# Attention in chunks, then a SoLU feed-forward: the opening's order of steps listed anew, g by another queue, two units of w_out scaled in place

## The chip, the cores and the metric

The kernel runs on one core of a Trainium2 chip. Its time is device time in microseconds (us), the median of the timed runs. Five engines each work through a list of instructions of their own, in order: TensorE (PE in the profile), VectorE (DVE), ScalarE (ACT), GpSimd (POOL) and SyncE (SP), which only issues transfers. An instruction waits until what it reads is written and what it overwrites is read.

## The reference

```python
# attention inside chunks of 64 tokens; batch 8, heads 8, seq 576, head_dim 64
scores = (1 / sqrt(D)) * q_c @ k_c.T          # per chunk and head, 64 x 64
attn = softmax(scores);  out = attn @ v_c
x = out with heads side by side               # 4608 tokens x 512
# feed-forward
h = x @ w_in                                  # 512 -> 1024
sm = softmax(h);  solu = h * sm
ln = (solu - mean(solu)) / sqrt(var(solu) + 1e-6) * g_ln
result = ln @ w_out                           # 1024 -> 512
```

w_in, w_out and g_ln are as they come; the weights reach the kernel as 64-bit floats and are turned into 32-bit ones on the chip.

## The kernel before

The 4608 tokens are 36 tiles of 128, two chunks each. A tile goes through: load q, k, v; q and k transposed; scores; softmax; attention transposed; values (which gives x transposed); product with w_in; SoLU; z transposed; product with w_out; store. Most products are taken in pieces: an operand is split into a high part of the float32r type and what is left of it, and three products (low weight, high, low of the data) add up in PSUM. Tiles 0 and 1 multiply the full 32-bit weights by plain float32 instead (FM = 2), before the parts exist.

**Units of weights.** w_in comes as units 0 to 3, w_out as units 4 to 7, 1 MB each. `load_pair` (line 144, step P) issues the transfer, unit 0 in two halves (P0, P1). `unit_scale` (167, step c) clamps the upper word, on VectorE or GpSimd, and then scales it on ScalarE. `unit_round` (183, step C) shifts by three bits and then adds the lower word, both on VectorE. `unit_high` (200, step t) writes the high part on ScalarE; for w_out it is multiplied by g on the way. `unit_rest` (213, step D:unit:half) writes what is left, on GpSimd for the halves in SUB_POOL (two instructions for w_out, a multiplication by g and a subtraction), else on VectorE in one.

**Steps of a tile.** n loads q and k, v loads v. N:i:0 and N:i:1 transpose q and k of tile i on TensorE into a PSUM bank, and the step's second mention copies the bank out (VectorE for the pairs in NV_DVE, else ScalarE). S: scores. A: VectorE takes the maximum and subtracts, the second mention has ScalarE's exponential. B: sum and reciprocal on VectorE, second mention the normalization (GpSimd for the tiles in NORM_POOL). T: attention transposed, then copied out. V: values on TensorE, then x copied out by ScalarE, the third mention the low part by VectorE. M: product with w_in (M:0 in four mentions, a unit each). X: VectorE's maximum of the product, then ScalarE's exponential. Y: VectorE's product, then an affine pass by ScalarE, or GpSimd for the tiles in MEAN_POOL. R: variance. z:i:x: half of z transposed on TensorE, high part by ScalarE, low part by VectorE. F: a third of an output product. o: store. Z, U, K, Q, q: the later tiles' transposes by VectorE and their loads. W: two small products on the identity that nothing reads. g loads the vector g, G transposes it and writes it for use.

**The order.** The opening, up to tile 4, is the string START (line 19): its words are called in order (line 815), each word being a step; a step with several parts goes one part on at each mention. Every engine gets its instructions in the order in which the words make them; that order is kept. Two words on different engines do not wait for each other unless data or a buffer ties them. PSUM gives the copies, transposes and output products two banks in turn (`bank`, line 116); `ph` holds one product with w_in at a time, so M of a tile follows the last read of the tile before, by Y. From tile 5 on a loop (line 838) makes one tile a turn; the change does not touch it.

Of the kernel before, what the change touches and what calls it, by code (L numbers as in the profile page):

```python
# [12 lines left out]
AF = mybir.ActivationFunctionType  # L13
# [3 lines left out]


START = """
W:41 W:42 n:0 n:1 N:0:1 N:0:0 N:0:0 N:0:1 N:1:0 n:2 S:0 N:2:1 N:1:0 A:0 A:0 P0 P1 P:2 N:1:1 B:0  # L20
P:1 c:0 c:2 N:1:1 W:43 c:0 N:2:0 S:1 W:44 W:45 W:46 N:2:1 N:2:0 n:3 c:2 C:0 A:1 A:1 C:0 B:0 c:1
B:1 S:2 T:0 N:3:0 T:0 W:47 g W:4 c:1 N:3:0 A:2 v:0 C:2 N:3:1 P:3 G P:4 t:0 V:0 N:3:1 n:4 C:1 B:1
G V:0 A:2 S:3 C:1 C:2 T:1 B:2 B:2 c:3 c:3 M:0 t:2 M:0 A:3 C:3 T:1 M:0 v:1 A:3 C:3 c:4 B:3 M:0
N:4:1 X:0 t:1 N:4:0 c:4 n:5 N:4:1 T:2 v:2 B:3 N:4:0 n:6 X:0 V:1 C:4 v:3 P:5 P:6 D:1:0 T:2 Y:0
S:4 T:3 C:4 N:5:0 V:1 A:4 t:3 A:4 P:7 T:3 D:1:1 M:1 t:4 N:5:1 D:3:1 B:4 D:2:1 N:5:0 D:0:1 D:2:0
D:0:0 Y:0 N:5:1 V:2 N:6:1 D:3:0 v:4 D:4:0 N:6:0 c:5 B:4 D:4:1 V:2 S:5 X:1 n:7 N:6:1 X:1 V:2 Y:1
z:0:1 N:6:0 V:3 z:0:1 c:5 R:0 A:5 z:0:0 C:5 A:5 z:0:0 V:3 C:5 M:2 z:0:1 T:4 c:6 B:5 z:0:0 V:3
Q:2 S:6 t:5 c:6 N:7:0 T:4 X:2 C:6 V:4 q:8 v:5 N:7:0 B:5 n:8 D:5:1 c:7 D:5:0 T:5 X:2 Y:2 C:6 T:5
F c:7 Y:2 t:6 C:7 N:7:1 C:7 N:7:1 D:6:1 D:6:0 M:3 F t:7 D:7:0 A:6 V:4 N:8:0 V:4 D:7:1 R:2 q:8
Y:1 N:8:0 V:5 S:7 X:3 Z:2 X:3 N:8:1 Y:3 A:7 N:8:1 A:6 q:8 q:8 F z:1:0 z:1:0 R:1 A:7 B:6 v:6  # L30
z:1:0 M:4 V:5 B:7 B:6 Y:3 U:6 o:0 B:7 Z:3 z:1:1 U:7 z:1:1 v:7 X:4 o:0 X:4 F z:1:1 Y:4 R:3 F K:9
F o:1 Y:4 o:1 V:5 R:4
"""


# [23 lines left out]
def chunk_attention_then_solu_ffn(  # L59
# [10 lines left out]
    nc = tc.nc  # L70

    B, H, S, D = q.shape
    DM, FF = H * D, g_ln.shape[0]
    P = 128
# [3 lines left out]
    G = S // 32  # L78
# [4 lines left out]
    assert FF == 32 * 32  # L83


    NV_DVE = ((0, 1), (1, 0), (2, 1), (4, 0), (6, 1), (9, 1),)
    MEAN_POOL = (3, 4,)
    CL_DVE = (0, 3, 4,)
    TV_DVE = (3,)
    SUB_POOL = ((0, 0), (0, 1), (1, 0), (1, 1), (2, 0), (2, 1), (3, 0), (3, 1), (7, 0), (7, 1),)  # L90
    NORM_POOL = (0, 1, 2, 3, 4, 5, 6, 7,)
    SH_POOL = ()
    XV_DVE = ()
    FM = 2
    MS = nc.gpsimd
    ORD = 5
# [12 lines left out]
    pe, dve, act, pool, sync = (  # L109
        order.engine(e)  # L110
        for e in (nc.tensor, nc.vector, nc.scalar, nc.gpsimd, nc.sync)
    )
# [12 lines left out]
    g_sb = const.tile([P, NFC], F32, name="g_sb")  # L125
    g_row = const.tile([NFC, P], F32, name="g_row")
# [40 lines left out]
    def unit_scale(x):  # L167
# [32 lines left out]
    def unit_high(x):  # L200
        kind, m = UNITS[x]
        a = scaled[x]
        if kind == "in":
            top = wi_h[:, m, :].rearrange("p (x n) -> p x n", x=2)
            act.copy(top, a)
        else:
            top = wo_h[:, 2 * m:2 * m + 2, :]
            for y in range(2):
                g = g_sb[:, 2 * m + y:2 * m + y + 1]
                act.activation(top[:, y], a[:, y], AF.Copy, scale=g)  # L210
        tops[x] = top

    def unit_rest(x, y):

        kind, m = UNITS[x]
        a, top = scaled[x], tops[x]
        g = None
        if kind == "in":
            low = wi_l[:, m, y * HALF:(y + 1) * HALF]
        else:  # L220
            low = wo_l[:, 2 * m + y, :]
            g = g_sb[:, 2 * m + y:2 * m + y + 1]
        of, part = a[:, y], top[:, y].bitcast(F32)
        if (x, y) in SUB_POOL:
            if g is not None:
                pool.tensor_scalar(out=of, in0=of, scalar1=g, scalar2=None, op0=ALU.mult)
            pool.tensor_tensor(out=low, in0=of, in1=part, op=ALU.subtract)
        elif g is None:
            dve.tensor_tensor(out=low, in0=of, in1=part, op=ALU.subtract)
        else:  # L230
            dve.scalar_tensor_tensor(
                out=low, in0=of, scalar=g, in1=part, op0=ALU.mult, op1=ALU.subtract
            )
# [5 lines left out]
    QT, KT, V, QS, KS = {}, {}, {}, {}, {}  # L239
# [98 lines left out]
    def turn_natural(i, x):  # L338
# [25 lines left out]
    def attn(i, part):  # L364
        return (sx, sy)[i % 2 if order.on else part][:, :, part]
# [46 lines left out]
    def softmax_b(i):  # L412
# [15 lines left out]
    def attn_transpose(i):  # L428
# [148 lines left out]
    def solu_b(i):  # L577
# [8 lines left out]
        yield  # L586
        if i not in MEAN_POOL:
            act.activation(z, z, AF.Identity, scale=-float(FF), bias=zsum)
# [156 lines left out]
        sync.dma_start(*early[1])  # L745

    def load_g():
        sync.dma_start(g_row, g_ln.rearrange("(a p) -> a p", p=P))

    def turn_g():  # L750
        pt = bank()[:, :NFC]
# [48 lines left out]
    def product():  # L800
# [135 lines left out]
```

## Time and profile before

| what | value |
|---|---|
| median of 3 runs | 476.63 us (476.55 to 477.74) |
| the profiled execution | 477.58 us, span 475.8 us |
| TensorE | busy 463.6 us, 97% of the span |
| VectorE | 369.1 us, 78% |
| ScalarE | 250.0 us, 53% |
| GpSimd | 160.8 us, 34% |
| chain that ended last | PE 91%, DVE 3%, DMA 2%, SyncE's queue 2% |

Busy time is the time in which an engine has an instruction under way. The span runs from the first instruction to the last, and the device's time has a little around it. A row of the timeline gives start, duration, engine, operation, what is written from what, shapes, the count of merged instructions, and in brackets the idle time before with what ended it. The program's names are those of the code: `w_a` is a unit being worked, `wi_l`/`wo_l` what is left of w_in/w_out, `wi_h`/`wo_h` the high parts, `po` a bank, `sx` the scores, `sy` the values, `ph` the product with w_in. Every row has line 50, since a helper at that line records every instruction.

### The profile page before, as it was taken

The numbers are of one execution on the slowest core, as the hardware profiler recorded it, in microseconds if no ns is written. First come the engines' busy times: TensorE is split into PE (matmuls) and PEld (weight loads), VectorE is DVE, ScalarE is ACT, GpSimd is POOL, SyncE is SP. The second block draws the span as 40 slices with busy tenths as digits, with TensorE's granted clock in tenths as the row PEclk, the third lists the DMA queues.
The fourth block names the chain that finished last, engine by engine and source line by source line (L and its number), as shares of the span: only waits on it lengthen the run. The fifth ranks groups of instructions, "written<-read, shape, count | busy, mean of one in ns | idle before, by whom it ended". The sixth has DMA issues, their size and how long they took to land.

```text
span 475.8 us, 10988 instructions
## 1 busy us (share of the span) xinstructions
PE 463.6 (97%) x4193; PEld 379.1 (80%) x4193; DVE 369.1 (78%) x511; ACT 250.0 (53%) x402; POOL 160.8 (34%) x305
## 2 busy tenths in 40 slices
PE   6799999999999999999999999999999999999996
PEld 5655888888888888888888888888888888888876
DVE  2799988798888787878788878787879797944430
ACT  2565885546464646464545454555555555554451
POOL 0438557350505050505050505032505050513300
PEclk9899999999999999999999999999999999999999
DMA  9999887877887877687358596959644435433211
GB/s 227 299 246 312 159 141 143 200 181 155 184 159 174 155 179 139 161 161 171 82 143 162 136 174 157 178 131 179 150 106 118 105 95 129 110 89 112 67 44 45
DMA packets 192996, 72.05 MB, mean 151 GB/s; under 512 B 177128, under 2 KB 177648, under 8 KB 192560
## 3 DMA queue, kind: packets, MB, share of 16 engines
q1 hardware_dynamic: 186528, 58.63, 55.4%
q0 software_dynamic: 6272, 12.60, 10.1%
q8 instruction: 33, 0.54, 0.5%
q14 instruction: 19, 0.16, 0.1%
q10 hardware_dynamic: 144, 0.13, 0.1%
HBM read 36.70 MB, written 9.44 MB: 97 GB/s over the span
## 4 chain that ended last, share of the span: by engine, by line
PE 91%; DVE 3%; DMA 2%; SPq 2%; issue 1%; ACT 0%; DVEq 0%; ACTq 0%
PE po L50 42%; PE ph L50 41%; PE sx L50 4%; PE sy L50 3%; DMA nat_z<-in_q_dram 2%; SPq L50 2%; DVE w_a L50 1%; DVE h_nmax L50 0%; DVE z L50 0%; ACT z L50 0%; DVE e L50 0%; DVE qT L50 0%; ACT z_h L50 0%; DVE s_nmax L50 0%; DVE s_sum L50 0%
## 5 line engine op out<-in xcount | busy, mean ns | idle before, releaser
L50 PE MATMUL po<-wo_l,z_h 128*128 128x512 f32 x280 | 110.9, 396 | 0.1
L50 PE MATMUL po<-wo_h,z_l 128*128 128x512 f32 x280 | 109.3, 391 | 0.0
L50 PE MATMUL po<-wo_h,z_h 128*128 128x512 f32 x280 | 109.3, 390 | 0.0
L50 ACT ACTIVATE z<-ph,h_nmax 128x1024 f32<-128x1024 f32 x36 | 40.2, 1116 | 131.6 <-DVE h_nmax L50 131.5
L50 PE MATMUL ph<-wi_l,x_h 128*128 128x512 f32 x272 | 106.1, 390 | 0.0
L50 PE MATMUL ph<-wi_h,x_h 128*128 128x512 f32 x272 | 105.8, 389 | 0.0
L50 POOL TENSOR_TENSOR u<-ssq,eps 128x1 f32<-128x1 f32 x36 | 6.8, 190 | 218.9 <-ACT sq L50 218.9
L50 POOL DMA_DIRECT2D z_t<-z_b x136 | 67.9, 506 | 16.6 <-DVE z_b L50 11.6
L50 PE MATMUL ph<-wi_h,x_l 128*128 128x512 f32 x272 | 72.7, 389 | 0.0
L50 DVE TENSOR_REDUCE h_nmax<-ph 128x1 f32<-128x1024 f32 x36 | 44.0, 1222 | 34.7 <-PE ph L50 34.7
L50 PEld LDWEIGHTS po<-wo_l,z_h 128*128 128x128 f32 x280 | 52.5, 188 | 11.9 <-ACT z_h L50 0.5
L50 PEld LDWEIGHTS po<-wo_h,z_l 128*128 128x128 f32 x280 | 52.6, 188 | 11.3 <-DVE z_l L50 0.4
L50 PEld LDWEIGHTS po<-wo_h,z_h 128*128 128x128 f32 x280 | 52.6, 188 | 10.4
L50 PEld LDWEIGHTS ph<-wi_l,x_h 128*128 128x128 f32 x272 | 51.1, 188 | 10.8 <-issue 0.2
L50 PEld LDWEIGHTS ph<-wi_h,x_l 128*128 128x128 f32 x272 | 51.0, 188 | 10.6
L50 PEld LDWEIGHTS ph<-wi_h,x_h 128*128 128x128 f32 x272 | 51.1, 188 | 10.5
L50 DVE TENSOR_TENSOR z_l<-z_t,z_h 128x1024 fp32r<-128x1024 f32 (+1 forms) x35 | 40.8, 1164 | 20.7 <-ACT z_h L50 20.7
L50 DVE SCALAR_TENSOR_TENSOR z<-ph,z 128x1024 f32<-128x1024 f32 x36 | 44.1, 1224 | 15.0 <-ACT z L50 15.0
L50 ACT ACTIVATE z<-z,z_sum 128x1024 f32<-128x1024 f32 x34 | 39.2, 1153 | 22.7 <-DVE z L50 21.6
L50 DVE STREAM_TRANSPOSE z_b<-z 128x1024 f32<-128x1024 f32 x33 | 39.9, 1210 | 6.1 <-ACT z L50 3.1
L50 ACT ACTIVATE o_sb<-po,r 128x512 f32<-128x512 f32 (+1 forms) x36 | 24.3, 675 | 28.4 <-POOL r L50 20.8
L50 ACT ACTIVATE sq<-z 128x1024 bf16<-128x1024 f32 x36 | 37.5, 1043 | 2.5 <-POOL z L50 2.5
(88 smaller groups left out, 624.5 us busy)
## 6 DMA issues: line engine op xcount, KB each, us to landing
out_dram<-o_sb SPq DMA_DIRECT2D x35, 256.0 KB, 2.5
z_t<-z_b SPq DMA_DIRECT2D x128, 64.0 KB, 3.1
z_t<-z_b POOLq DMA_DIRECT2D x128, 64.0 KB, 2.8
q_st<-in_q_dram SPq DMA_DIRECT2D x96, 72.0 KB, 3.2
k_st<-in_k_dram SPq DMA_DIRECT2D x96, 72.0 KB, 2.8
v_sb<-in_v_dram SPq DMA_DIRECT2D x27, 256.0 KB, 4.4
w_raw<-in_moe_w_out_dram SPq DMA_DIRECT2D x4, 1024.0 KB, 7.9
attn_t<-a_b POOLq DMA_DIRECT2D x60, 64.0 KB, 3.5
```

The lines of the kernel that those rows point to most:

```text
L50: ins = make(*args, **kwargs)
```

## The change

START is replaced as a whole by another order of the same 262 words (each word as often as before). The first transfers become: q and k of tile 0, unit 1, tile 1, unit 0, tile 2, unit 2, v of tile 0, unit 3, tile 3. Before they were tiles 0, 1, 2, units 0, 2, 1, tile 3, g, v of tile 0, unit 3. The lists that choose engines change with it. g is loaded by ScalarE's queue instead of SyncE's. For units 4 and 7 (GM_ACT) ScalarE multiplies the unit by g in place and then copies it to the high part, and the rest is a plain subtraction.

```diff
 START = """
-W:41 W:42 n:0 n:1 N:0:1 N:0:0 N:0:0 N:0:1 N:1:0 n:2 S:0 N:2:1 N:1:0 A:0 A:0 P0 P1 P:2 N:1:1 B:0
-P:1 c:0 c:2 N:1:1 W:43 c:0 N:2:0 S:1 W:44 W:45 W:46 N:2:1 N:2:0 n:3 c:2 C:0 A:1 A:1 C:0 B:0 c:1
-B:1 S:2 T:0 N:3:0 T:0 W:47 g W:4 c:1 N:3:0 A:2 v:0 C:2 N:3:1 P:3 G P:4 t:0 V:0 N:3:1 n:4 C:1 B:1
...
+n:0 N:0:0 P:1 c:1 N:0:1 N:0:0 n:1 P0 P1 N:0:1 S:0 W:41 c:1 n:2 N:1:0 W:45 A:0 P:2 v:0 N:1:0
+N:1:1 C:1 A:0 N:1:1 W:44 P:3 C:1 n:3 W:43 S:1 t:1 n:4 W:42 n:5 B:0 B:0 T:0 T:0 A:1 c:0
+W:47 W:46 A:1 B:1 c:0 B:1 N:2:0 W:4 C:0 c:2 N:2:1 N:2:0 N:2:1 C:0 V:0 v:1 c:2 V:0 P:5 S:2
+A:2 T:1 v:3 t:0 A:2 D:1:1 g c:3 c:5 c:3 M:0 T:1 C:2 C:2 M:0 C:3 C:3 N:3:0 M:0 N:3:1
+N:3:0 N:3:1 D:0:0 N:4:0 B:2 M:0 t:3 B:2 N:4:1 N:4:0 S:3 N:4:1 N:5:0 X:0 X:0 A:3 T:2 N:5:0 V:1 V:1
+S:4 P:4 v:2 Y:0 A:4 n:6 A:3 B:3 N:5:1 T:2 M:1 P:6 B:3 n:7 Y:0 R:0 z:0:0 N:5:1 A:4 Q:2
+B:4 t:2 D:2:0 D:1:0 T:3 c:5 D:2:1 C:5 C:5 X:1 z:0:0 B:4 T:3 V:2 z:0:0 v:4 S:5 G G v:5
+c:4 D:3:0 V:2 X:1 V:2 z:0:1 Y:1 N:6:0 N:6:0 A:5 z:0:1 c:4 t:5 C:4 C:4 D:0:1 P:7 V:3 V:3 V:3
+N:6:1 D:3:1 c:6 M:2 N:6:1 z:0:1 c:6 D:5:1 T:4 N:7:1 D:5:0 t:4 C:6 S:6 X:2 T:4 A:5 D:4:0 X:2 D:4:1
+B:5 B:5 Y:2 c:7 V:4 V:4 N:7:1 F q:8 T:5 Y:2 M:3 Y:1 c:7 T:5 C:6 C:7 t:6 D:6:0 C:7
+t:7 D:6:1 A:6 v:6 q:8 Z:2 q:8 N:7:0 N:7:0 F n:8 q:8 V:4 D:7:0 A:6 D:7:1 X:3 z:1:0 z:1:0 F
...
-    NV_DVE = ((0, 1), (1, 0), (2, 1), (4, 0), (6, 1), (9, 1),)
-    MEAN_POOL = (3, 4,)
-    CL_DVE = (0, 3, 4,)
-    TV_DVE = (3,)
-    SUB_POOL = ((0, 0), (0, 1), (1, 0), (1, 1), (2, 0), (2, 1), (3, 0), (3, 1), (7, 0), (7, 1),)
-    NORM_POOL = (0, 1, 2, 3, 4, 5, 6, 7,)
+    NV_DVE = ((5, 1), (8, 0), (9, 1))
+    MEAN_POOL = (2, 3, 4)
+    CL_DVE = (1, 7)
+    TV_DVE = ()
+    GM_ACT = (4, 7)
+    SUB_POOL = ((0, 1), (1, 0), (2, 0), (3, 0), (3, 1), (4, 1), (5, 0), (6, 0), (7, 0))
+    NORM_POOL = (0, 1, 4, 5, 6)
-    XV_DVE = ()
+    XV_DVE = (0,)
...
-                act.activation(top[:, y], a[:, y], AF.Copy, scale=g)
+                act.activation(
+                    a[:, y] if x in GM_ACT else top[:, y], a[:, y], AF.Copy, scale=g
+                )
+            if x in GM_ACT:
+                act.copy(top, a)
...
-            g = g_sb[:, 2 * m + y:2 * m + y + 1]
+            if x not in GM_ACT:
+                g = g_sb[:, 2 * m + y:2 * m + y + 1]
...
-        sync.dma_start(g_row, g_ln.rearrange("(a p) -> a p", p=P))
+        nc.scalar.dma_start(g_row, g_ln.rearrange("(a p) -> a p", p=P))
```

## Rows read from the trace of the kernel before

**Rows 1.** Busy time by stretch: stretch, length, each engine's busy us, clock, DMA.

```profile
23.58:83.45 59.87, 58.24 (x582) 42.67 (x581) 54.36 (x74) 43.03 (x71) 36.67 (x37) 0.99 0.90 201
83.45:455.00 371.55, 371.48 (x3348) 307.11 (x3347) 298.75 (x414) 192.07 (x309) 117.74 (x253) 1.00 0.63 142
```

**Rows 2.** TensorE in order of time, 20 to 84 us.

```profile
20.34 0.63 PE L50 MATMUL po<-ident,nat_z 128*128 128x128 f32 x4 [2.42 <-DMA nat_z<-in_q_dram]
...
22.39 1.06 PE L50 MATMUL po<-ident,nat_z 128*128 128x128 f32 x4
...
23.58 1.02 PE L50 MATMUL sy<-attn_t,v_sb 64*64 64x64 f32 x32
...
38.01 7.10 PE L50 MATMUL ph<-w_a,x_f 128*128 128x512 f32 x16 [0.94 <-DVE z L50]
...
46.11 1.09 PE L50 MATMUL po<-ident,nat 128*128 128x128 f32 x8
47.13 0.69 PE L50 MATMUL sx<-kT,qT 64*64 64x64 f32 x32
47.76 0.66 PE L50 MATMUL po<-ident,z 128*128 128x128 f32 x4
...
49.65 0.47 PE L50 MATMUL ph<-wi_l,x_h 128*128 128x512 f32 x1
...
55.20 0.60 PE L50 MATMUL po<-ident,e 128*128 128x128 f32 x4
...
83.45 0.39 PE L50 MATMUL ph<-wi_l,x_h 128*128 128x512 f32 x1
```

**Rows 3.** Busy time by stretch, the last two numbers: DMA share, GB/s.

```profile
4.00:8.00 4.00, 2.74 (x12) 2.28 (x12) 0.69 (x1) 0.59 (x1) 0.00 (x0) 1.00 1.38 218
12.00:17.00 5.00, 4.47 (x77) 3.80 (x78) 4.28 (x8) 2.91 (x4) 1.94 (x2) 1.00 0.98 398
18.00:21.00 3.00, 0.66 (x6) 0.69 (x7) 2.83 (x6) 1.60 (x2) 2.35 (x2) 0.99 0.84 146
```

**Rows 4.** SyncE's queue in order of time: start, time to issue.

```profile
13.74 3.63 SPq L50 DMA_DIRECT2D g_row<-in_moe_g_ln_dram  x1
```

**Rows 5.** VectorE in order of time, 34 to 45 us.

```profile
34.90 1.82 DVE L50 TENSOR_SCALAR w_a<-w_a 128x1024 uint32<-128x1024 uint32 x1
...
37.79 2.29 DVE L50 SCALAR_TENSOR_TENSOR w_a<-w_raw,w_a 128x1024 uint16<-128x1024 uint32 x1
...
44.11 1.76 DVE L50 SCALAR_TENSOR_TENSOR wo_l<-w_a,g_sb,wo_h 128x512 fp32r<-128x512 f32 x1
```

**Rows 6.** GpSimd in order of time, single instructions at 35.2 and 39.5 us.

```profile
34.90 1.27 POOL L50 TENSOR_TENSOR wi_l<-w_a,wi_h 128x512 fp32r<-128x512 f32 x1
...
38.84 2.33 POOL L50 TENSOR_TENSOR wi_l<-w_a,wi_h 128x512 fp32r<-128x512 f32 x1
```

**Rows 7.** VectorE in order of time, 45 to 58 us.

```profile
45.79 1.21 DVE L50 TENSOR_REDUCE h_nmax<-ph 128x1 f32<-128x1024 f32 x1
...
49.42 0.69 DVE L50 TENSOR_REDUCE s_nmax<-sx 128x8 f32<-128x512 f32 x1
...
50.82 0.68 DVE L50 TENSOR_SCALAR w_a<-w_a 128x1024 uint32<-128x1024 uint32 x1
51.54 1.37 DVE L50 SCALAR_TENSOR_TENSOR w_a<-w_raw,w_a 128x1024 uint16<-128x1024 uint32 x1
52.78 0.69 DVE L50 TENSOR_TENSOR z_l<-po,z_h 128x512 fp32r<-128x512 f32 x1
...
57.14 1.41 DVE L50 SCALAR_TENSOR_TENSOR wo_l<-w_a,g_sb,wo_h 128x512 fp32r<-128x512 f32 x2
```

**Rows 8.** ScalarE in order of time, 29 to 32 us.

```profile
29.64 0.58 ACT L50 COPY attn_t<-po 128x512 f32<-128x512 f32 x1
30.11 0.63 ACT L50 ACTIVATE e<-e 128x512 f32<-128x512 f32 x1
30.64 1.04 ACT L50 CAST wi_h<-w_a 128x1024 fp32r<-128x1024 f32 x1
```

More of the change, by code (lines that the diff above doesn't have):

```diff
@@ L19 @@
 START = """
-W:41 W:42 n:0 n:1 N:0:1 N:0:0 N:0:0 N:0:1 N:1:0 n:2 S:0 N:2:1 N:1:0 A:0 A:0 P0 P1 P:2 N:1:1 B:0
-P:1 c:0 c:2 N:1:1 W:43 c:0 N:2:0 S:1 W:44 W:45 W:46 N:2:1 N:2:0 n:3 c:2 C:0 A:1 A:1 C:0 B:0 c:1
-B:1 S:2 T:0 N:3:0 T:0 W:47 g W:4 c:1 N:3:0 A:2 v:0 C:2 N:3:1 P:3 G P:4 t:0 V:0 N:3:1 n:4 C:1 B:1
[L23 to L32, printed above, removed]
+n:0 N:0:0 P:1 c:1 N:0:1 N:0:0 n:1 P0 P1 N:0:1 S:0 W:41 c:1 n:2 N:1:0 W:45 A:0 P:2 v:0 N:1:0
[9 more added lines that the diff above has]
+t:7 D:6:1 A:6 v:6 q:8 Z:2 q:8 N:7:0 N:7:0 F n:8 q:8 V:4 D:7:0 A:6 D:7:1 X:3 z:1:0 z:1:0 F
+B:6 V:5 S:7 v:7 R:2 z:1:0 o:0 z:1:1 B:6 X:3 Y:3 U:6 z:1:1 Y:3 z:1:1 A:7 R:1 R:3 A:7 B:7
+B:7 F Z:3 M:4 X:4 X:4 N:8:1 U:7 Y:4 F F N:8:1 Y:4 V:5 o:1 o:1 N:8:0 V:5 N:8:0 o:0
+K:9 R:4
 """
```

## The prediction

> **What bounds the kernel now.** I read the busy time by stretch first, then TensorE's instructions in order of time, then the other engines' rows around each of its waits. From 83.45, where the loop's first product starts [rows 2], to 455 us TensorE works 371.48 of 371.55 us [rows 1]. Before that, from tile 0's first product of attention and values (V:0 at 23.58) to 83.45, it works 58.24 of 59.87 [rows 1]. Nothing after 83.45 is changed, so the question is at what time the loop's first product starts. The opening has its waits before 38 us: a pause of 2.42 ends at 20.34 with a load of q, and one of 0.94 ends at 38.01 [rows 2]. The multiset of steps is the same in both lists: TensorE does the same work, and only waits can come or go.
>
> **The change part by part.**
>
> *The front, a gain.* V:0 needs v of tile 0. The new list puts in front of it only tiles 0 to 2 of q and k (six transfers of 256 KB) and units 1, 0 and 2 of w_in (3 MB). By the rates in [rows 3], 218 GB/s for the 256-byte pieces of q and k and 398 for weights, that is 6 x 1.2 + 3 x 2.6 = 15.0 us. The first tile's q was used at 5 us in both lists, so transfers start near 3, and v (1.2 more) is there at 19.2. A hole in the transfers like that of 18 to 21 (146 GB/s, [rows 3]) would add up to 1.5. I take V:0 at 19.3; bounds 18.7 and 20.8. By then TensorE has done two quarters of transposes (tile 3's) and one set of scores (S:2) less than before at 23.58. By [rows 2] these are 2 x 0.51 (46.11 to 47.13 is two) and 0.63 (47.13 to 47.76): 1.65. With no wait behind V:0 the loop would start at 19.3 + 58.24 + 1.65 = 79.2, which is 4.25 sooner than 83.45.
>
> *TensorE's clock.* The pause ahead of V:0 is as long as the one before: tile 2's q and k are there at about 3 + 7.2 + 5.2 = 15.4, and their eight transposes are done by 17. In [rows 2] four transposes that start at 20.34 take 0.63, and four at 22.39 take 1.06: after that pause the engine fell to the lower of its two levels, 1.2 GHz, and was back by 25. If it falls again, some 3.4 us of work take twice as long: 0 to 1.7. I take 0.8, since part of it lies where tile 0's product would wait for units 2 and 3 anyway.
>
> *Small edits.* g goes to ScalarE's queue. On SyncE its issue took 3.63 us, queued behind large transfers [rows 4]; ScalarE's queue is empty then, so I take 0.4, bounds 0 and 3.6. It hides in ScalarE's slack (43.03 busy of 59.87, [rows 1]). Two extra copies of 128x1024 for units 4 and 7 (0.94 each, start to start in [rows 8]) hide there too, and GpSimd loses three multiplications. VectorE's own list changes little: three copies of transposed q or k, one of attention and one clamp go away, three normalizations, one subtraction of weights and tile 0's x copy come, all pieces of 0.65 to 0.7 (the 512-column rows of [rows 7]). No loss or gain is taken for these.
>
> *The stretch behind tile 0's product, a loss.* [rows 5] and [rows 6] belong together. VectorE's shift, usually 0.68 (at 50.82, [rows 7]), took 1.82 from 34.90, while a GpSimd subtraction ran from 34.90 to 36.17: it ended 0.55 behind that one. The add of the low word, usually 1.37, took 2.29 from 37.79 and ended at 40.08; the GpSimd subtraction issued at 38.84 took 2.33 instead of 1.27 and ended 1.09 behind it. So these two engines take turns: an instruction of this kind waits for the whole one of the other engine. The low half of w_out, two of which take 1.41 at 57.14, took 1.76 alone from 44.11, with both inputs in SBUF; the plain subtractions of the new list have the same inputs, and I count them like it. VectorE's reads of PSUM (the reduction at 45.79, inside GpSimd's row) show nothing of it.
>
> The Trainium skill, "SBUF — State Buffer", section "Who interferes with whom", says the same: VectorE with two SBUF inputs, or in a two-port mode, contends with a GpSimd instruction that reads SBUF, and whoever is first keeps the ports for the whole instruction. It names the plain subtraction among these, which no row here shows on VectorE beside GpSimd's work; were it free of the turns, the sum below would be about 1 lower.
>
> Before, GpSimd's row of eight subtractions (33.7 to 47) met four VectorE instructions of this kind, and TensorE had work in hand. In the new list GpSimd's row is D:2:0, D:1:0, B:4, c:4, D:3:0, D:0:1, D:3:1, c:6, two for D:5:0, D:4:1. VectorE meets it with D:2:1, both halves of C:5, both of C:4, D:5:1, the first half of C:6 and D:4:0, and TensorE waits at two places. Let e be the end of M:0.
>
> First place, z:0:1. TensorE behind e: N:4:1, S:3, N:5:0, T:2, V:1, S:4, N:5:1 = 4.0, M:1 7.1 [rows 2], then z:0:0, T:3, V:2, S:5, G = 2.45: it wants z:0:1 at e+13.5. That needs a PSUM bank, free when VectorE has done z:0:0's subtraction. ScalarE: X:0's reduction ends at e+1.25; then ten activations up to c:5, five of 1024 columns at about 1.0, five of 512 at about 0.5 and a small one [rows 8] = 7.7. So t:2 ends at e+7.95 and c:5 at e+8.95. VectorE then needs D:2:1 0.7, C:5 0.7 + 1.25, X:1 1.15, z:0:0 0.65 (start to start in [rows 7]). Without turns: C:5 ends near e+11, X:1 starts with M:1's end at e+11.1, z:0:0 is done at e+12.9: no wait. With turns D:2:0 goes first at t:2 (1.27), D:2:1, D:1:0 (1.27), the shift, B:4 (1.05), the add: C:5 ends at 7.95 + 1.27 + 0.7 + 1.27 + 0.7 + 1.05 + 1.25 = e+14.2 and z:0:0 at e+16.0. That is 2.5 late; if one of the turns falls the other way, 1.4. I take 2.3, bounds 0 and 3.2.
>
> Second place, the first third of tile 0's output product (F), which reads D:4:0. Let s be the start of z:0:1. TensorE: z:0:1, N:6:0, V:3, N:6:1 2.2, M:2 5.55 (49.65 to 55.20, [rows 2]), T:4, N:7:1, S:6, V:4 2.3: F at s+10.05. VectorE, from the end of Y:1 at s+1.85 (X:1 ends at s-0.65, then two passes over 1024 columns, 1.2 each with their waits): A:5 1.4 (49.42 to 50.82), C:4 1.95, two PSUM subtractions 1.25, D:5:1 0.7, C:6's shift 0.7 = s+7.85; X:2 behind M:2 1.15, D:4:0 0.7: s+9.7. It fits by 0.35 without turns. GpSimd has eight pieces here, 8 x 1.25 = 10 us back to back, so each of the five VectorE instructions of the kind finds it busy. Two follow another directly and wait a full piece (1.25); three wait half of one (0.65): 4.4, less 0.35. I take 3.7, bounds 0 and 6.
>
> Later, C:6, C:7 and D:6:1 meet D:6:0, D:7:0 and tile 2's mean on GpSimd in the same way, and the second third of F reads D:6:0. I take 1.3, bounds 0 and 3.
>
> **Sum.** -4.25 + 0.8 + 2.3 + 3.7 + 1.3 = +3.9 us. The profiled run took 477.58 us (span 475.8, 1.8 around it), 0.95 above the median of the runs shown, 476.63. On the profiled run the sum gives 481.5; on the median, against which I predict, 480.5.
>
> **Rivals.**
> - *The turns are absorbed* (faster, 0.23). In the other order GpSimd's pieces fall beside VectorE's PSUM reads, and the slacks (0.6 and 0.35) hold. For it: each of the places fits without turns, and VectorE was busy 54.36 of 59.87 us before [rows 1] with only 1.6 us of waits on TensorE. Against: a row of 10 us back to back leaves no room to miss. Time: 476.63 - 4.25 + 0.8 = 473.2; with half of the smaller losses 475. It decides at 3.45 us of waits behind V:0: below that the change is a gain.
> - *Waits eat the gain and no more* (0.12): one of the two places holds, the other loses 2.5 to 4: 475.5 to 478.
> - *v is late as well* (0.13): transfers are the limit in any order, so listing them sooner doesn't land them sooner. V:0 at 20.8, g's issue holds ScalarE 3.6 us while c:3 stands behind it, and the stalls take the clock down once more (1.7): 476.63 + 3.9 + 1.5 + 0.9 + 1.0 = 484.
> - Likeliest (0.52): 480.5, its own range 478.2 to 483.
>
> **Chances.** A change of 0.3%, 1.4 us, is about what a measurement can tell from none. Slower is the likeliest case, the late one and a small part of the one between: 0.66. Faster is the first rival and a little of the second: 0.24. Same: 0.10. The range leaves out the best end of the first rival and the worst of the third: 474.3 to 483.5.
>
> **What would show it.** V:0 near 19.3 and M:1 starting at 33 to 35 instead of 38.01 would show the front right. A wait of about 2 us on TensorE between G and z:0:1, released by VectorE, and one of 3 to 4 us ahead of the first third of F, released by D:4:0, would show the turns; the shift and add of C:5 and C:4 at 1.5 to 2.6 us would show their cause. The loop's first product should start near 87.4. If it starts before 82 with C:5 and C:4 at their usual 0.68 and 1.37, the turns were mis-sized and the prediction falls. If V:0 stands beyond 21, the transfers were misjudged.

## The result, and the profile after

The changed kernel takes 479.91 us (median of six runs, 479.47 to 481.40), the kernel before 477.14 beside it (six runs, 476.55 to 478.06): a ratio of 1.0063, 95% interval 1.0043 to 1.0083. It is slower, by 2.8 us. The profiled execution took 480.99, its span is 479.2 (before: 477.58 and 475.8).

The loop's first product starts at 86.73 instead of 83.45 [rows 2], and from there on TensorE has no wait worth naming in either kernel. So all of the loss is in the opening. TensorE of the changed kernel in order of time (start, duration, what; in brackets the idle time before and what ended it):

```profile
21.11 0.33 PE L51 MATMUL sy<-attn_t,v_sb 64*64 64x64 f32 x4 [1.23 <-DMA v_sb<-in_v_dram]
...
23.90 5.09 PE L51 MATMUL ph<-w_a,x_f 128*128 128x512 f32 x8
...
29.27 1.88 PE L51 MATMUL ph<-w_a,x_f 128*128 128x512 f32 x4
...
37.68 7.11 PE L51 MATMUL ph<-w_a,x_f 128*128 128x512 f32 x16
...
48.47 0.66 PE L51 MATMUL po<-ident,z 128*128 128x128 f32 x4 [1.56 <-DVE z_l L51]
...
58.15 0.69 PE L51 MATMUL sy<-attn_t,v_sb 64*64 64x64 f32 x32 [0.29 <-ACT attn_t L51]
...
59.46 0.47 PE L51 MATMUL po<-wo_l,z_h 128*128 128x512 f32 x1 [0.62 <-DVE wo_l L51]
...
71.95 0.50 PE L51 MATMUL po<-wo_l,z_h 128*128 128x512 f32 x1 [0.19 <-DVE wo_l L51]
...
74.48 0.66 PE L51 MATMUL po<-ident,z 128*128 128x128 f32 x4 [0.47 <-DVE z_l L51]
...
86.73 0.48 PE L51 MATMUL ph<-wi_l,x_h 128*128 128x512 f32 x1
```

V:0 starts at 21.11, 2.47 sooner than before, but M:1 starts at 37.68 against 38.01: the gain of the front is used up before tile 1's product. Then come five waits, 3.13 us together. Busy time by stretch of the changed kernel (stretch, length, then busy us of TensorE, its weight loads, VectorE, ScalarE and GpSimd, the granted clock, the transfers' share and GB/s):

```profile
21.00:25.00 4.00, 3.52 (x70) 2.66 (x71) 3.61 (x5) 1.45 (x2) 2.84 (x3) 0.81 1.06 268
25.00:30.00 5.00, 5.00 (x13) 2.30 (x13) 4.93 (x5) 3.03 (x5) 0.81 (x1) 0.81 1.08 175
23.49:26.90 3.41, 3.41 (x8) 1.76 (x7) 3.31 (x5) 3.35 (x4) 1.16 (x2) 0.50 1.01 184
21.11:86.73 65.62, 61.93 (x622) 44.70 (x622) 60.63 (x78) 45.69 (x75) 40.80 (x39) 0.97 0.95 197
37.68:86.73 49.05, 45.74 (x415) 34.49 (x414) 46.10 (x60) 35.91 (x61) 37.27 (x36) 1.00 0.92 185
```

and of the kernel before, its own stretch at the lower clock and the stretch that answers to the last of these:

```profile
20.93:24.35 3.42, 3.42 (x42) 3.06 (x44) 1.51 (x4) 2.12 (x3) 0.00 (x0) 0.50 0.90 299
38.01:83.45 45.44, 45.41 (x413) 34.79 (x413) 40.94 (x56) 32.66 (x56) 31.48 (x33) 1.00 0.87 188
```

The account: from V:0 to the loop it is 65.62 us instead of 59.87 [rows 1]. TensorE's busy time grew by 61.93 - 58.24 = 3.69, of which 1.65 is the work that was moved behind V:0; the other 2.04 is more busy time for the same work. The clock accounts for some 1.3 of it: 0.50, the lower level, is granted for 3.41 us from 23.49 on, which costs 1.7 (two quarters of tile 0's product take 5.09 where 1.88 each is usual), and in the kernel before the same costs 0.4 behind V:0, from 23.58 to 24.35. Where the remaining 0.7 comes from is not shown; 0.33 of it lies behind M:1 (45.74 busy instead of 45.41), where the clock is 1.00. Its idle time went from 1.63 to 3.69. Together -2.47 + 1.65 + 2.04 + 2.06 = +3.28, as seen. The second half of the stretch, from M:1 on, is 3.61 longer, and VectorE is busy 46.10 of 49.05 there, where it was 40.94 of 45.44.

Why VectorE: its rows around C:5 and C:4, the shift and the add of units 5 and 4 of the weights,

```profile
42.92 1.41 DVE L51 TENSOR_SCALAR w_a<-w_a 128x1024 uint32<-128x1024 uint32 x1 [0.27 <-ACT w_a L51]
44.37 2.35 DVE L51 SCALAR_TENSOR_TENSOR w_a<-w_raw,w_a 128x1024 uint16<-128x1024 uint32 x1
46.61 1.21 DVE L51 TENSOR_REDUCE h_nmax<-ph 128x1 f32<-128x1024 f32 x1
47.73 0.68 DVE L51 TENSOR_TENSOR z_l<-po,z_h 128x512 fp32r<-128x512 f32 x1
...
51.66 1.28 DVE L51 TENSOR_SCALAR w_a<-w_a 128x1024 uint32<-128x1024 uint32 x1
52.98 2.18 DVE L51 SCALAR_TENSOR_TENSOR w_a<-w_raw,w_a 128x1024 uint16<-128x1024 uint32 x1
...
58.65 0.67 DVE L51 TENSOR_TENSOR wo_l<-w_a,wo_h 128x512 fp32r<-128x512 f32 x1
```

and GpSimd's beside them:

```profile
42.01 3.46 POOL L51 TENSOR_TENSOR wi_l<-w_a,wi_h 128x512 fp32r<-128x512 f32 x2 [0.62 <-DVE s_rinv L51]
45.43 2.15 POOL L51 TENSOR_TENSOR e<-e,s_rinv 128x512 f32<-128x512 f32 x1
...
48.63 3.77 POOL L51 TENSOR_TENSOR wi_l<-w_a,wi_h 128x512 fp32r<-128x512 f32 x3
52.37 1.56 POOL L51 TENSOR_SCALAR w_a<-w_raw 128x1024 f32<-128x1024 f32 x1
53.91 2.65 POOL L51 TENSOR_SCALAR w_a<-w_a,g_sb 128x512 f32<-128x512 f32 x1
56.64 3.82 POOL L51 TENSOR_TENSOR wo_l<-w_a,wo_h 128x512 fp32r<-128x512 f32 x2
```

C:5 takes 3.8 us in place of 2.05 [rows 7], the reduction X:1 stands behind it, z:0:0's low part (47.73) behind that, and z:0:1 waits 1.56 for it. Beside it GpSimd is slowed too: 2.15 for a normalization that takes 1.04 alone. Second, C:4 stood at 34.90 and 37.79 before, its shift ahead of M:1 and its add beside it [rows 5]; now unit 4's transfer is issued at 35.16 instead of 20.68, and all of C:4 stands inside the stretch, from 51.66 on.

### The profile page after: what moved, and what is told of

Its sections match the earlier page's. It is cut to its first block, busy times and chain, and to the rows that moved or that the text cites. A ratio compares the mean times of both kernels' runs of the same rounds, so it can differ in the third digit from the quotient of the medians.

```text
span 479.2 us, 10997 instructions
## 1 busy us (share of the span) xinstructions
PE 464.0 (97%) x4193; PEld 378.6 (79%) x4193; DVE 372.5 (78%) x511; ACT 252.3 (53%) x406; POOL 163.0 (34%) x303
## 4 chain that ended last, share of the span: by engine, by line
PE 85%; DVE 7%; SPq 3%; ACT 2%; DMA 1%; issue 1%; DVEq 0%; ACTq 0%
PE po L51 40%; PE ph L51 38%; PE sx L51 4%; SPq L51 3%; PE sy L51 3%; DVE w_a L51 3%; DMA v_sb<-in_v_dram 1%; DVE h_nmax L51 1%; DVE wo_l L51 1%; ACT z L51 1%; DVE z L51 1%; DVE z_l L51 0%; DVE x_l L51 0%; DVE e L51 0%; DVE s_sum L51 0%
## 5 line engine op out<-in xcount | busy, mean ns | idle before, releaser
L51 POOL DMA_DIRECT2D z_t<-z_b x136 | 67.9, 506 | 19.3 <-DVE z_b L51 14.3
L51 ACT ACTIVATE z<-z,z_sum 128x1024 f32<-128x1024 f32 x33 | 38.1, 1155 | 22.7 <-DVE z L51 21.6
```

The source lines that it names most:

```text
L51: ins = make(*args, **kwargs)
```

## The experiments

One line a kernel: V:0, M:1, the stretch from M:1 to the loop's first product, that product (from one profiled execution each), and the ratio to the kernel before with its 95% interval.

| kernel | V:0 | M:1 | stretch | loop | ratio |
|---|---|---|---|---|---|
| before | 23.58 | 38.01 | 45.44 | 83.45 | |
| changed | 21.11 | 37.68 | 49.05 | 86.73 | 1.0063 (1.0043 to 1.0083) |
| e_v_first | 18.82 | 35.55 | 49.27 | 84.82 | 1.0032 (1.0020 to 1.0044) |
| e_warm | 20.60 | 36.45 | 48.10 | 84.55 | 1.0054 (1.0036 to 1.0072) |
| e_early_rest | 22.17 | 38.39 | 47.15 | 85.54 | 1.0042 (1.0027 to 1.0058) |
| e_rest_dve | 20.48 | 38.51 | 53.52 | 92.03 | 1.0150 (1.0131 to 1.0169) |
| e_free_pool | 20.55 | 37.79 | 47.61 | 85.40 | 1.0057 (1.0037 to 1.0076) |
| e_free_v | 17.20 | 34.45 | 48.79 | 83.24 | 1.0034 (1.0019 to 1.0050) |
| e_order | 21.79 | 45.83 | 55.14 | 100.97 | 1.0361 (1.0332 to 1.0390) |
| e_lists | 22.97 | 38.14 | 50.28 | 88.42 | 1.0134 (1.0112 to 1.0156) |
| e_shed | 20.15 | 36.82 | 49.00 | 85.82 | 1.0056 (1.0035 to 1.0076) |
| e_shed_v | 18.93 | 37.63 | 48.39 | 86.02 | 1.0053 (1.0034 to 1.0071) |
| e_c5_v | 17.25 | 34.57 | 47.91 | 82.48 | 1.0020 (1.0006 to 1.0034) |
| e_best | 18.14 | 35.34 | 48.60 | 83.94 | 1.0021 (1.0001 to 1.0040) |

### The front: e_v_first and e_warm

```diff
-A:0 P:2 v:0 N:1:0
+A:0 v:0 P:2 N:1:0
```

> The changed kernel with v of tile 0 issued ahead of unit 2 instead of behind it; nothing else. Theory T (the gain of the front went to a late v and to the lower clock behind the pause before V:0; turns of VectorE and GpSimd took the rest): v is there near 18.5 instead of 22.1, V:0 starts near 19.9 without the pause of 1.23, the granted clock stays at full speed from 21 to 30, tile 0's product runs its first two quarters in 3.6 instead of 5.09, and M:1 starts near 35.4 instead of 37.68 (34.7 to 36.7). The waits behind it stay about as they are: time 1 to 3 below the changed kernel, 477.6. Rival (transfers are the limit in any order): unit 2 lands 1.2 later, the third quarter of tile 0's product waits for it, M:1 starts at 37 to 38.5, time within 0.7 of the changed kernel.

Theory T held on the trace; V:0 came sooner than forecast (18.82 against 19.9). TensorE of this kernel:

```profile
18.82 0.69 PE L51 MATMUL sy<-attn_t,v_sb 64*64 64x64 f32 x32
...
22.22 3.70 PE L51 MATMUL ph<-w_a,x_f 128*128 128x512 f32 x8 [1.11 <-DVE x_f L51]
27.03 1.98 PE L51 MATMUL ph<-w_a,x_f 128*128 128x512 f32 x4 [0.68 <-DVE w_a L51]
...
46.42 0.66 PE L51 MATMUL po<-ident,z 128*128 128x128 f32 x4 [1.64 <-DVE z_l L51]
```

M:1 at 35.55 (35.4 was expected), the clock at 1.00, the first two quarters in 3.70, and the wait behind M:1 unmoved (1.64). Half of the loss is gone (by the ratios 0.31%, some 1.5 us, in T's 1 to 3, though the two intervals just touch and the time was 479.08, not T's 477.6), with two words of the order exchanged. Unit 2, now behind v, costs a wait of 0.68.

```diff
-C:0 V:0 v:1
+C:0 W:40 W:48 W:49 W:50 V:0 v:1
```

> The changed kernel with eight more small products on the identity (four words W) just ahead of V:0, in the pause of 1.23 in which TensorE waits for v. T: the pause is what the clock falls behind; with it filled, V:0 starts at 21.1 to 21.4 as before, the granted clock from 21 to 30 is 1.00 instead of 0.81, the first two quarters of tile 0's product take 3.6 instead of 5.09; the third quarter can start only when the round of unit 2 ends (28.3 in the changed kernel), so M:1 starts 0.7 to 1.4 sooner, at 36.5, and the time is 478.9 (478.4 to 479.3). Rival (the clock falls for what the engine did long before, or the list of VectorE sets the start of M:1 anyway): clock still 0.81, or M:1 at 37.5 to 37.9 and the time within 0.4 of the changed kernel.

With the engine kept at work through the pause, the clock is at 1.00 in this profile (columns as above):

```profile
21.00:25.00 4.00, 3.64 (x69) 2.48 (x70) 3.07 (x5) 2.43 (x3) 2.27 (x2) 1.00 1.01 232
25.00:30.00 5.00, 4.35 (x16) 2.10 (x15) 4.93 (x6) 2.32 (x4) 0.38 (x1) 1.00 0.99 193
```

M:1 starts at 36.45, 1.23 sooner (0.7 to 1.4 expected), of which 0.51 is V:0's own (20.60). In the time it can't be told from the changed kernel, as the rival had it: the median is 480.16, not T's 478.9, and the profiled run was the quickest of its six (478.82 to 481.57).

That the pause is what the clock falls behind, this does not show. e_order, further below, left a longer pause empty, and its clock stayed as well (TensorE's row, then the stretch with the columns as above):

```profile
21.79 0.33 PE L51 MATMUL sy<-attn_t,v_sb 64*64 64x64 f32 x4 [1.75 <-DMA v_sb<-in_v_dram]
```

```profile
21.00:30.00 9.00, 7.05 (x82) 4.21 (x83) 7.77 (x10) 4.96 (x7) 3.91 (x3) 1.00 1.11 235
```

Nor is the clock the same in every run of a kernel: averaged over a whole run, the granted clock lies between 0.991 and 1.000 in the six of the changed kernel, and between 0.995 and 1.000 in those of e_warm.

### The turns: e_early_rest, e_rest_dve, e_free_pool

```diff
-g c:3 c:5 c:3 M:0
+g c:3 c:3 M:0
-C:3 C:3 N:3:0 M:0
+C:3 C:3 t:2 N:3:0 M:0
-M:0 t:3 B:2
+M:0 t:3 D:2:0 D:1:0 D:0:1 D:3:0 D:3:1 c:5 B:2
-B:4 t:2 D:2:0 D:1:0 T:3
+B:4 T:3
-c:4 D:3:0 V:2
+c:4 V:2
-C:4 D:0:1 P:7
+C:4 P:7
-N:6:1 D:3:1 c:6
+N:6:1 c:6
```

> The changed kernel with the same instructions on the same engines, only five subtractions of GpSimd (halves of units 0 to 3 of w_in) and the step t:2 that the one of unit 2 needs put some 10 us sooner, where GpSimd idles from 25.8 to 38.4, and the clamp c:5 behind them. T (turns): the shift and the add of C:5 take 0.68 and 1.32 instead of 1.41 and 2.35, the wait of 1.56 ahead of z:0:1 goes, and of the later ones (0.29, 0.62, 0.19, 0.47) about half; the loop's first product starts 1.6 to 2.8 sooner than 86.73 and the time is 477.7 (477.0 to 478.4). Rival L (VectorE's and ScalarE's own lists are too long in front of z:0:0's low part, GpSimd has no share in it): C:5 still ends behind 46, a wait of over 1.0 stays ahead of z:0:1, time 479.3 to 480.2.

The stretch got 1.9 shorter, as T had it, but not at the place it named, and with v later in this run the ratio, 1.0042, missed T's 477.7. VectorE:

```profile
43.14 1.53 DVE L51 TENSOR_SCALAR w_a<-w_a 128x1024 uint32<-128x1024 uint32 x1
44.71 2.16 DVE L51 SCALAR_TENSOR_TENSOR w_a<-w_raw,w_a 128x1024 uint16<-128x1024 uint32 x1
```

and GpSimd of the same kernel:

```profile
42.84 1.29 POOL L51 TENSOR_TENSOR e<-e,s_rinv 128x512 f32<-128x512 f32 x1 [0.74 <-DVE s_rinv L51]
44.10 1.56 POOL L51 TENSOR_SCALAR w_a<-w_raw 128x1024 f32<-128x1024 f32 x1
```

The next two pieces of GpSimd's list, B:4 and the clamp c:4, moved up into the place of those taken away, and C:5 waited for them. I had taken the partner away without asking who is next in its queue. A wait of 1.01 stayed. By its marks the rival L came true (C:5 ended at 46.87, the wait stayed above 1.0, the time was 479.75); by its reason it did not, since the shift and the add each ended 0.5 and 1.2 behind a piece of GpSimd's. The next two kernels were made to part the two.

```diff
-SUB_POOL = ((0, 1), (1, 0), (2, 0), (3, 0), ...
+SUB_POOL = ((0, 1), (3, 0), ...
```

> The changed kernel with the two subtractions D:2:0 and D:1:0, which GpSimd does at 42.0 to 45.4 beside C:5, given to VectorE in the same place: VectorE has two instructions of 0.69 more ahead of C:5, GpSimd two fewer. T (turns): C:5 starts 1.4 later but takes 2.0 instead of 3.8, so that it ends where it did or up to 0.5 sooner, and the wait ahead of z:0:1 stays within 0.6 of 1.56; time 479.5 (478.8 to 480.0). L (VectorE's own list is what is too long): C:5 ends 1.4 later, the wait ahead of z:0:1 grows to 2.6 to 3.0 and the time to 481.0 to 481.5.

Both theories missed the size. VectorE:

```profile
42.80 3.67 DVE L51 TENSOR_TENSOR wi_l<-w_a,wi_h 128x512 fp32r<-128x512 f32 x3
46.39 1.77 DVE L51 TENSOR_SCALAR w_a<-w_a 128x1024 uint32<-128x1024 uint32 x1
48.19 2.25 DVE L51 SCALAR_TENSOR_TENSOR w_a<-w_raw,w_a 128x1024 uint16<-128x1024 uint32 x1
```

Each subtraction given to VectorE became one more instruction that takes turns (3.67 for three, 2.07 without), GpSimd's later pieces filled the place again, and the wait ahead of z:0:1 grew to 4.46. That it grew by more than the 1.4 of the added work speaks against L's plain sum of durations, and that C:5 stayed at 4.0 against my T. Not all of the time is VectorE's: around that wait, from 51.47 to 58.30, TensorE's granted clock is 0.50, and of the 4.47 by which the stretch is longer than the changed kernel's, 2.32 is busy time and 2.15 idle time.

So that GpSimd is really idle beside C:5, this kernel ties it to a transfer (on top of e_early_rest):

```diff
-X:1 z:0:0 B:4 T:3
+X:1 z:0:0 T:3
-N:6:1 c:6 M:2
+N:6:1 c:6 B:4 M:2
-c:4 V:2 X:1 V:2 z:0:1 Y:1 N:6:0
+V:2 X:1 V:2 z:0:1 Y:1 c:4 N:6:0
-CL_DVE = (1, 7)
+CL_DVE = (1, 4, 7)
```

> The kernel e_early_rest with GpSimd kept idle while VectorE rounds unit 5 (C:5): the normalization B:4 moved behind the clamp c:6, which waits for its transfer until 49, and the clamp c:4 given to VectorE behind Y:1; nothing else. The earlier runs showed that the place of the subtractions taken away is filled by B:4 and c:4, so that C:5 waited all the same. T (turns): with GpSimd idle from 42 to 49, the shift and the add of C:5 take 0.68 and 1.32, C:5 ends 2.0 to 2.2 behind its start at 42 to 43, and the wait of 1.0 to 1.6 ahead of z:0:1 is under 0.2; of the later waits about half go; the loop's first product starts 2 to 3 sooner than in the changed kernel (86.73), time 1.5 to 3 below it, ratio to the kernel before 1.000 to 1.003. Rival L (the shift and the add are slow for another reason, a transfer that writes beside them or the form of unit 5): they take 1.4 and 2.2 with GpSimd idle as well, the wait stays above 1.0, the ratio above 1.004.

VectorE with GpSimd idle from 41.50 to 47.47:

```profile
42.55 0.68 DVE L51 TENSOR_SCALAR w_a<-w_a 128x1024 uint32<-128x1024 uint32 x1
43.27 1.31 DVE L51 SCALAR_TENSOR_TENSOR w_a<-w_raw,w_a 128x1024 uint16<-128x1024 uint32 x1
...
46.08 0.68 DVE L51 TENSOR_TENSOR z_l<-po,z_h 128x512 fp32r<-128x512 f32 x1
```

This settles the mechanism: same instructions, same unit, 0.68 and 1.31, and no wait ahead of z:0:1 at all (the 1.56 is gone). It does not settle the time. Later waits of 0.53 (for ScalarE's copy, whose queue is held by the later c:4), 0.81 and 0.41 took its place, the stretch was 47.61, and V:0 stood behind a pause of 2.56 with the clock at 0.50 to 0.81 after it. The ratio missed my 1.000 to 1.003.

### Order and lists apart: e_order and e_lists

```diff
-NV_DVE = ((5, 1), (8, 0), (9, 1))
...
+NV_DVE = ((0, 1), (1, 0), (2, 1), (4, 0), (6, 1), (9, 1),)
...
```

> The changed kernel's order and g's queue with all lists that choose engines as they were in the kernel before (no unit scaled in place). T (the order is what costs: a late v and GpSimd's row beside C:5): the front is as in the changed kernel (V:0 at 21 to 22, M:1 at 37 to 38.5), C:5 meets the same GpSimd row, and the leftovers of units 4 to 6 are all VectorE's: no better than the changed kernel, ratio 1.006 to 1.013. Rival (the lists are at fault, the order is good): ratio below 1.001.

> The kernel before with the changed kernel's lists (engines of copies, clamps, normalizations and leftovers, two units scaled by g in place) and g by ScalarE's queue, in the order of before. T (the order is what costs): V:0 at 23.0 to 23.8 and M:1 at 37.5 to 38.5 as in the kernel before, ratio 0.998 to 1.003. Rival (the lists are at fault): ratio 1.005 or more.

(e_lists is the changed kernel with the old START.) Neither half is the culprit: each alone is worse than both together. In e_order both theories missed (T had a ratio up to 1.013 and M:1 up to 38.5, which came at 45.83), in e_lists T did and the rival's 1.005 or more came; V:0 was where T had it (21.79 and 22.97), without telling the time. With the old lists under the new order, B:2's normalization is GpSimd's and stands behind the clamp c:5, which waits for a transfer; TensorE waits 6.87 for it. TensorE of e_order:

```profile
42.26 1.11 PE L51 MATMUL po<-ident,e 128*128 128x128 f32 x4 [6.87 <-POOL e L51]
```

GpSimd of e_order:

```profile
38.89 1.09 POOL L51 TENSOR_SCALAR w_a<-w_raw 128x1024 f32<-128x1024 f32 x1 [13.99 <-DMA w_raw<-in_moe_w_out_dram]
...
41.17 1.04 POOL L51 TENSOR_TENSOR e<-e,s_rinv 128x512 f32<-128x512 f32 x1
```

Lists and order are one schedule; a test that exchanges one of them measures the mismatch.

### Both losses at once: e_free_v, e_shed, e_shed_v, e_c5_v, e_best

e_free_v is e_free_pool with v:0 ahead of P:2.

> The kernel e_free_pool with v of tile 0 issued ahead of unit 2 as well. T: the two losses are separate, so the gains add up: M:1 starts near 35.5 as in e_v_first, without the wait ahead of z:0:1; the loop's first product starts near 82.5 (81.3 to 84), 1 sooner than in the kernel before (83.45), and the ratio to that is 0.998 (0.995 to 1.001). Rival (the weights of w_out, whose transfers stay where they are, become the limit): the third of the output product that reads units 4 and 5 waits 1 to 2 for them, ratio 1.001 to 1.004.

M:1 at 34.45, a microsecond sooner than T had it, but the stretch grew back to 48.79 and the ratio, 1.0034, is the rival's: the sum does not hold. (The loop's 83.24 is that of one of the quickest of its twelve runs, 477.56 of 477.44 to 480.29.) VectorE had 18.27 of 20 us busy from 40 to 60, which gave theory B: VectorE's length sets the stretch. e_shed cuts it (on top of e_early_rest):

```diff
-NV_DVE = ((5, 1), (8, 0), (9, 1))
+NV_DVE = ((8, 0), (9, 1))
-CL_DVE = (1, 7)
+CL_DVE = (1,)
-SUB_POOL = ((0, 1), (1, 0), (2, 0), (3, 0), ...
+SUB_POOL = ((0, 1), (1, 0), (2, 0), (2, 1), (3, 0), ...
-Y:0 R:0 z:0:0
+Y:0 z:0:0
-B:4 T:3 c:5 D:2:1 C:5 C:5 X:1 z:0:0 B:4 T:3
+B:4 T:3 D:2:1 c:5 R:0 C:5 C:5 X:1 z:0:0 T:3
-c:4 V:2 X:1
+V:2 X:1
-A:5 z:0:1 c:4
+A:5 c:6 c:4 B:4 z:0:1 c:4
-N:6:1 c:6 M:2
+N:6:1 M:2
```

> The kernel e_early_rest with VectorE's own list in the stretch behind M:1 cut: half a unit's leftover (D:2:1) and the clamp of unit 7 go to GpSimd, one copy of transposed k (N:5:1) to ScalarE, 0.64 to 0.69 each; GpSimd is kept off C:5 as in e_free_pool, but the clamp c:4 stays on it, behind c:6; the variance R:0 of tile 0 moves behind c:5 on ScalarE. Theory B (a new one, from the traces so far: from M:1 to the loop's first product VectorE is the bound, that stretch took 49.05 where VectorE's durations add up to 48.75, and 47.61 with 46.76 in e_free_pool; turns lengthen its instructions and steps moved behind M:1 add to them): VectorE's durations in the stretch add up to 44.5 to 46, the stretch takes 45.6 to 46.6, M:1 starts at 37 to 38.5, the loop's first product at 83.0 to 84.8, ratio to the kernel before 0.998 to 1.003. Rival (the waits stand where TensorE meets ScalarE's copies or late transfers of w_out, VectorE's length is beside the point): the stretch still takes over 47.3, ratio above 1.004.

Theory B's forecast fell. VectorE was busy only 15.78 of 20 us from 40 to 60, and the stretch took 49.00: c:4, put behind c:6 and its late transfer, made TensorE wait 1.33 for a copy in ScalarE's queue and 0.95 for a leftover of GpSimd's. Since the edit brought these two waits with it, what VectorE's length alone is worth stays open. e_shed_v (v:0 ahead of P:2, x of tile 0 copied by ScalarE, P:7 ahead of v:5) did no better:

> The kernel e_shed with v of tile 0 issued ahead of unit 2, its x copied by ScalarE ahead of c:2 instead of by VectorE, and unit 7 issued ahead of v of tile 5. Theory B: the front's gain stands now, since the stretch behind M:1 holds: M:1 at 34.0 to 35.5, the stretch 45.6 to 46.8, the loop's first product at 80 to 82, ratio 0.992 to 0.998. Rival (with M:1 sooner the transfers of w_out or VectorE take it back, as in e_free_v, whose stretch grew from 47.61 to 48.79): the stretch over 47.5, ratio 0.999 to 1.004.

There the loads of tile 3's q, listed behind all this, came late (0.86 on TensorE), M:1 started at 37.63, and the stretch took 48.39.

Last, C:5 put ahead of B:4 by data, so that GpSimd has nothing to do beside it and no clamp is held up:

```diff
-A:0 P:2 v:0 N:1:0
+A:0 v:0 P:2 N:1:0
-Y:0 R:0 z:0:0 N:5:1 A:4 Q:2
-B:4 T:3 c:5 D:2:1 C:5 C:5 X:1
+Y:0 z:0:0 c:5 R:0 C:5 C:5 N:5:1 A:4 Q:2
+B:4 T:3 D:2:1 X:1
-Y:1 N:6:0 N:6:0 A:5 z:0:1 c:4 t:5 C:4 C:4 P:7
+Y:1 c:4 N:6:0 N:6:0 C:4 C:4 A:5 z:0:1 t:5 P:7
```

(the moves of e_early_rest are in it too).

> The changed kernel with v of tile 0 ahead of unit 2 and five GpSimd subtractions and t:2 sooner (as in e_early_rest), and C:5 put ahead of B:4's sum on VectorE (c:5 ahead of the variance R:0 on ScalarE), so that GpSimd's next two pieces, B:4 and c:4, can't start before C:5 is done, by data and by order; C:4 ahead of A:5 behind it, so that it ends before D:5:0 starts on GpSimd. No engine's work changes and no clamp is held up by a later transfer, which is what cost e_free_pool and e_shed their gain (a wait of 0.5 to 1.3 for ScalarE's copy ahead of V:4). T (turns at C:5 and C:4 are what the stretch behind M:1 loses): C:5 and C:4 take 0.7 and 1.3 each, no wait ahead of z:0:1, under 0.5 ahead of the first third of F, the stretch from M:1 to the loop's first product takes 45.6 to 46.8 instead of 49.05, M:1 starts at 35 to 36.6, the loop at 81 to 83.2, ratio to the kernel before 0.994 to 1.000. Rival (the engines' lists are too full: taken away at one place, the wait comes back at another, as in every run so far): the stretch takes over 47.5, ratio above 1.001.

C:5 and C:4 went as T said (C:4 took 0.69 and 1.39), the stretch (47.91) and the ratio as the rival said. VectorE:

```profile
39.40 0.69 DVE L51 TENSOR_SCALAR w_a<-w_a 128x1024 uint32<-128x1024 uint32 x1 [2.10 <-ACT w_a L51]
40.13 1.33 DVE L51 SCALAR_TENSOR_TENSOR w_a<-w_raw,w_a 128x1024 uint16<-128x1024 uint32 x1
```

GpSimd:

```profile
36.82 1.46 POOL L51 TENSOR_SCALAR w_a<-w_raw 128x1024 f32<-128x1024 f32 x1 [2.47 <-DMA w_raw<-in_moe_w_out_dram]
```

TensorE behind the loop's start:

```profile
89.51 0.30 PE L51 MATMUL sx<-attn_t,v_sb 64*64 64x64 f32 x2 [0.69 <-DMA out_dram<-o_sb]
90.14 0.63 PE L51 MATMUL sx<-attn_t,v_sb 64*64 64x64 f32 x27 [0.34 <-DMA attn_t<-a_b]
```

C:5 no longer waits for GpSimd but for unit 5, whose clamp waits 2.47 for its transfer, and 0.46 ahead of z:0:1 is left. The loop's first product starts at 82.48, 0.97 sooner than in the kernel before; seven us later TensorE waits 1.03 for transfers. So of the changed kernel's 0.63% this version gives back two thirds (1.0020).

e_best adds two edits:

```diff
-GM_ACT = (4, 7)
+GM_ACT = (4, 6, 7)
-N:3:1 D:0:0 N:4:0
+N:3:1 N:4:0
-Y:0 z:0:0 c:5
+Y:0 D:0:0 z:0:0 c:5
```

> The kernel e_c5_v, and unit 6 scaled by g in place as well (one multiplication on GpSimd less ahead of the second third of F, one copy on ScalarE more), and the leftover D:0:0 behind Y:0 on VectorE instead of ahead of B:2. T: 0.5 to 1.5 better than e_c5_v: the stretch 45.4 to 46.2, the loop's first product at 80 to 82, ratio to the kernel before 0.992 to 0.998. Rival: as in e_c5_v, ratio above 1.001.

1.0021: no different. Unit 5 landed at 38.72 in its profiled run, C:5 started at 41.02, and the wait ahead of z:0:1 was 1.23. No version here beats the kernel before.

## Why the prediction was right, and where its steps were not

The direction and the size held (480.5 predicted, 479.91 measured; +3.9 forecast, +2.8 measured), both with errors that cancel: the gain of the front was 2.45 instead of 4.25, and the waits were 3.69 instead of 7.3. With the front and the clock as I had them (-4.25 + 0.8), the waits that came would have made +0.2, no change at all. So that it is slower, and not the same, is in part luck; the mechanism, turns that hold VectorE ahead of z:0:1, is not.

- *The front, V:0 at 19.3.* It was 21.11, beyond the later bound. Mis-sized: unit 1's megabyte, first in the queue behind tile 0's q and k, landed 4.7 us behind them and unit 2 3.8 behind its predecessor, where I took 2.6. The gain was 2.45 and not 4.25. V:0 beyond 21 was the sign I had named for misjudged transfers, and M:1, wanted at 33 to 35, came at 37.68. That v could have come sooner is shown by e_v_first.
- *The clock, +0.8.* Some 1.3 more than in the kernel before, between my 0.8 and my bound of 1.7: it fell into the first two quarters of tile 0's product. What it falls behind is not shown (e_warm, e_order).
- *g by ScalarE's queue, 0.4.* Nothing: it was issued at 0.72, with the first transfer of all.
- *Other small edits, nothing.* GpSimd does not lose three multiplications, as I had it, but does two in either kernel (at 53.91 and 64.32 in the changed one); nothing was added up from that. The copies that ScalarE makes for units 4 and 7 did not all hide: the copy that V:4 waited 0.29 for, at 57.52, stood right behind unit 4's:

```profile
56.56 1.05 ACT L51 CAST wo_h<-w_a 128x1024 fp32r<-128x1024 f32 x1
```

- *First place, +2.3.* 1.56, by the mechanism named: C:5 at 1.41 and 2.35, X:1 and z:0:0's low part behind it. e_free_pool takes GpSimd away and the wait goes. D:1:1, a plain subtraction, took 1.50 beside GpSimd's clamp c:3 in place of 0.68, and ended 0.55 behind it: it takes turns too (its row and the clamp's below). The Trainium skill ("SBUF — State Buffer", "Who interferes with whom") names `tensor_tensor` with both inputs in SBUF, which this subtraction is, among what contends with GpSimd's reads; the trace agrees.

```profile
24.85 1.50 DVE L51 TENSOR_TENSOR wi_l<-w_a,wi_h 128x512 fp32r<-128x512 f32 x1
```

```profile
24.68 1.12 POOL L51 TENSOR_SCALAR w_a<-w_raw 128x1024 f32<-128x1024 f32 x1 [1.16 <-DMA w_raw<-in_moe_w_in_dram]
```

- *Second place, +3.7.* 0.62, and 0.29 ahead of V:4. Here the step failed. I let VectorE wait at each of five meetings. It did at C:4 (1.28 and 2.18), but at D:5:1, C:6's shift and D:4:0 it was GpSimd that waited: 2.65 for a multiplication, 3.82 for two subtractions. The Trainium skill says in the same section ("SBUF — State Buffer", "Who interferes with whom") that the order of issue decides who is held up; the trace agrees (the 2.65 was issued inside the add that ran from 52.98), and I had priced one direction only.
- *Later, +1.3.* 0.66 (0.19 and 0.47), both for VectorE, as named; that a turn is behind each is not shown.
- *"VectorE's own list changes little."* True of the whole, wrong for the stretch: C:4 (2.05 without turns), whose instructions had both started ahead of M:1, went behind it with its transfer. Added up over the instructions that start in the stretch, VectorE's durations above the shortest of each kind grew from some 2.7 to some 6.5 (turns), and what is left grew by some 2, about the length of C:4. That this want of slack is why taking a turn away gave back less than the wait (e_free_pool, e_c5_v) is likely but not shown: e_shed, which cut VectorE's work, brought waits of its own.
- Rivals: "the turns are absorbed" fell with the idle time of 3.69; "v is late as well" was right on V:0 and the clock, and wrong on g and on the size of the waits.

Left open: what part of the last 0.2% of e_c5_v is the wait for transfers in the loop's first turns, and what part the stretch. From M:1 to the loop the transfers' share was 0.92 in the changed kernel and 1.00 in e_c5_v; that a load listed sooner then makes another late, and that this is the floor under the kernel before, was not tried. In the time, the turns' share of the loss is open too: e_free_pool, without the wait of 1.56, can't be told from the changed kernel (1.0057 and 1.0063), and only v's place has been shown to move the time by itself.

## What to carry to other kernels

When a step is listed sooner, ask which transfer, which queue and which partner engine get its place: in e_v_first the v that came sooner cost a wait of 0.68 for unit 2, and the subtractions taken from GpSimd's queue were replaced by the next pieces within a microsecond. Price a shared resource by both engines' queues, and a stretch by the work that is moved into it, not by the whole list's sum. A clock that is kept up is worth something only as far as the next operand is there: in e_warm the third quarter of tile 0's product then waited 0.65 for unit 2.

## What the runs showed of the hardware that I had not expected

- The turns cost both sides: with C:5 and C:4 VectorE loses 1.8 and 1.4 us, and GpSimd's normalization beside them takes 2.15 for 1.04, its two subtractions 3.82 for 2.54. From M:1 to the loop GpSimd's durations lie some 7 us above their shortest, VectorE's some 6.5.
- With the same list of first transfers, V:0 stood at 20.15 to 22.17 in seven kernels, and the clock behind it at 0.50 to 1.00: 2 us of spread, though none of their edits is to the transfers ahead of it. It is about as large as the effects looked for; the table's times are of one profile each, and only the ratios rest on all runs.
- SyncE took 5.94 us to issue unit 0's two halves and 3.04 for unit 2: the loads listed after them were issued only when these were through. What holds an issue so long is not shown.
